# Attention scores of two experts as 64-row float32 products, with mask, scale and row minimum in one VectorE instruction

## The chip, the cores and the metric

The kernel runs on one core of a Trainium2 chip. The metric is the device time of one execution in microseconds (us).

## The reference, cut to what matters

Three layers follow one another: retention over 768 tokens (2 batches, 8 heads of 64), a feed-forward layer with 512 model columns and 2,048 hidden ones, and causal attention by four experts of head size 64, whose outputs are weighted by a gate that keeps the best two experts of each token. The change touches the attention alone:

```
scale = 1.0 / np.sqrt(Hd)
for e in range(E):
    q = x @ wq[e]
    k = x @ wk[e]
    v = x @ wv[e]
    scores = scale * (q @ k.transpose(0, 2, 1))
    causal = np.triu(np.ones((S, S), dtype=bool), 1)
    scores = np.where(causal, -1000000000.0, scores)
    scores = scores - scores.max(-1, keepdims=True)
    a = np.exp(scores)
    a /= a.sum(-1, keepdims=True) + 1e-09
    ye = a @ v @ wo[e]
```

## The kernel before, in words

The program is a list of steps (matmul groups, copies, transfers), each with an estimated cost, the buffers it reads and writes, and a priority. `Plan.issue` places them by a list schedule over estimated times when the program is built: a step is taken when its inputs are ready, its engine is free by the estimate and its new buffers have a place. The order found there is fixed for each engine; on the chip an engine runs its list in that order and waits where an input is late. Names in `QUEUES` share one order of allocation, so that all score, probability and transposed tiles are handed out in program order.

The attention has these steps, all in the last quarter of the execution.

- `q_proj` (line 747) makes queries and keys of one block of 384 tokens (TB) for two experts at once: 12 matmuls of 128x384 into one PSUM bank, expert 2p on partitions 0 to 63, expert 2p+1 on 64 to 127. Each expert's half then goes to tiles of its own. A query tile `QS` holds in one half the query rounded to float32r (ScalarE, L766, times 0.125), in the other half the remainder (VectorE, L768). A key is kept as the rounded `KH` (ScalarE, L773) and the remainder `KL` (VectorE, L775), and a transfer within SBUF (L779) copies each to the other 64 partitions. So a product with 128 rows against `KH` and another against `KL` give the float32 product of 64 rows.
- `q_val` (L793) makes the values and gate logits of 128 tokens, `gates` the gates.
- `a_scores` (line 841) takes one tile `qt` of 128 queries and two experts (`z` = 0, 1): nk = 128(qt+1) keys, so 128 to 768 columns; above 512 columns in two halves in two banks (`ways` = 2). Per expert: matmuls L863 and L864 (against `KH` and `KL`), then on VectorE a `copy_predicated` L870 that writes -1e9 over the future part of the last 128 columns in PSUM, a `tensor_reduce` L871 for the negated row maximum, on ScalarE the exponential L873 from PSUM to the SBUF tile `pr`, with the row sum as accumulator (a second small instruction reads it out). After both experts, VectorE inverts the sums (L879, L880) and GpSimd multiplies `pr` by inverse and gate (L885).
- `a_turn` transposes `pr` in 128x128 pieces on TensorE (L905); `COPY` (L335, on whichever of ScalarE and VectorE is free by the plan) takes four pieces at a time from PSUM to `pt` or `ptn`.
- `a_value` multiplies by the values (L924; 64 output columns, two experts side by side), `a_out` by `wo` (L948), and the result goes out.

Batch 0's attention is interleaved with batch 1's projections (L756, L793). In the profile a matmul's form is written rows*columns of the stationary operand: 128*128 is the whole array, 128*64 (L924) uses half of its columns, 64*128 half of its rows. The retention scores at the start (L435) are plain float32 products with 64 rows, for two heads in alternation; each float32 product stands as two records.

Of the kernel before, what the change touches and what calls it, by code (L numbers as in the profile page):

```python
# [26 lines left out]
U32 = mybir.dt.uint32  # L27
AF = mybir.ActivationFunctionType
OP = mybir.AluOpType
# [28 lines left out]
ROUNDED = {"x", "w", "w1", "S", "t", "h", "wq", "wk", "wv", "wo", "qk0", "qk1", "at"}  # L58
# [149 lines left out]
def region(base, size, n, space="S"):  # L208
    return [(space, base + i * size, size) for i in range(n)]
# [3 lines left out]
def retention_channel_mlp_mixture_attention(ctx: ExitStack, tc: tile.TileContext, a):  # L213
# [13 lines left out]
    future = cst.tile([128, C], U32, name="future")  # L227
# [66 lines left out]
    PL["qk0"] = region(o_r, 3 * KB, 12)  # L294
    PL["vv0"] = region(o_r + 36 * KB, KB, 6)
    PL["ob"] = region(o_r + 42 * KB, 2 * KB, 2)
    PL["qk1"] = region(o_h, 3 * KB, 12)
    PL["vv1"] = region(o_h + 36 * KB, KB, 6)
    PL["pr"] = region(o_xt, 3 * KB, 8)
    PL["pt"] = region(o_x, 6 * KB, 3)  # L300
    PL["ptn"] = region(o_x, 7 * KB // 2, 5)
# [13 lines left out]
    def new(n):  # L315
        return Buf(PL[n], n)
# [4 lines left out]
    def ACT(c, fn, r=(), w=()):  # L321
        P.add({"A": c}, lambda e: fn(), r, w)

    def DVE(c, fn, r=(), w=()):
        P.add({"V": c}, lambda e: fn(), r, w)
# [412 lines left out]
    QS, KH, KL, VV, LG, GT = {}, {}, {}, {}, {}, {}  # L738
    xkeys = lambda t: [(t, "k", k) for k in range(NK)]

    def q_alloc(b):
        for e in range(E):
            QS[b, e], KH[b, e], KL[b, e] = (new(f"qk{b}") for _ in range(3))
        for t in range(NC):
            VV[b, t] = new(f"vv{b}")

    def q_proj(b, j, n, p):
# [12 lines left out]
        for z in range(2):  # L760
            e = 2 * p + z
            own = slice(64 * z, 64 * z + 64)
            oth = slice(64 - 64 * z, 128 - 64 * z)
            if n == "wq":
                q = QS[b, e]
                ACT(0.39, lambda q=q, own=own: act.activation(f32r(q)[own, cs], f32(pa, TB)[own], AF.Copy, scale=0.125),  # L766
                    r=[pa], w=[(q, j, 0)])
                DVE(0.47, lambda q=q, own=own, oth=oth: dve.scalar_tensor_tensor(  # L768
                    f32r(q)[oth, cs], f32(pa, TB)[own], 0.125, f32(q)[own, cs], op0=OP.mult, op1=OP.subtract),
                    r=[pa, (q, j, 0)], w=[(q, j, 1)])  # L770
            else:
                kh, kl = KH[b, e], KL[b, e]
                ACT(0.39, lambda t=kh, own=own: act.activation(f32r(t)[own, cs], f32(pa, TB)[own], AF.Copy),  # L773
                    r=[pa], w=[(kh, j, 0)])
                DVE(0.47, lambda t=kl, h=kh, own=own: dve.tensor_tensor(f32r(t)[own, cs], f32(pa, TB)[own],  # L775
                                                                        f32(h)[own, cs], OP.subtract),
                    r=[pa, (kh, j, 0)], w=[(kl, j, 0)])
                for t in (kh, kl):
                    DMA(96e3, lambda t=t, own=own, oth=oth: sp.dma_start(f32(t)[oth, cs], f32(t)[own, cs]),  # L779
                        r=[(t, j, 0)], w=[(t, j, 1)])  # L780
# [60 lines left out]
    def a_scores(b, qt, p):  # L841
# [3 lines left out]
        PR = []  # L845
        P.bias -= (20, 40)[b]
        for z in range(2):
            e = 2 * p + z
            s, pr = new("ps2" if nk > 512 else "ps1"), new("pr")
            PR.append(pr)  # L850

            ways = 1 if nk <= 512 else 2
            wide = nk // ways

            def halves(ap, step):
                return ap[:, :ways * step].rearrange("p (a x) -> p a x", a=ways)[:, :, :wide]

            def mm(e=e, s=s):
                q = f32r(QS[b, e])[:, qt * C:(qt + 1) * C]
                for n in range(ways):  # L860
                    ks = slice(n * wide, (n + 1) * wide)
                    out = f32(s)[:, 512 * n:512 * n + wide]
                    pe.matmul(out, lhsT=q, rhs=f32r(KH[b, e])[:, ks], start=True, stop=False)  # L863
                    pe.matmul(out, lhsT=q, rhs=f32r(KL[b, e])[:, ks], start=False, stop=True)  # L864
            PE(2 * ways * max(0.107, wide * .4513e-3 + .015), mm, r=[(QS[b, e], j, 0), (QS[b, e], j, 1)] +
               [(t, jj, y) for t in (KH[b, e], KL[b, e]) for jj in range(j + 1) for y in range(2)], w=[s])

            def mx(s=s, z=z):
                end = 512 * (ways - 1) + wide
                dve.copy_predicated(f32(s)[:, end - C:end], future, negs)  # L870
                dve.tensor_reduce(f32(sm)[:, z:z + 1], halves(f32(s), 512), axis=mybir.AxisListType.XY, op=OP.max, negate=True)  # L871
            DVE(0.43 + nk * 1.05e-3, mx, r=[s, "future", "negs"], w=[s, (sm, z)])
            ACT(act_c(nk) + .18, lambda s=s, pr=pr, z=z: act.activation(  # L873
                halves(f32(pr), wide), halves(f32(s), 512), AF.Exp, bias=f32(sm)[:, z:z + 1], scale=1.0,
                accum_out=f32(sm)[:, 2 + z:3 + z]), r=[s, (sm, z)], w=[pr, (sm, 2 + z)])
# [104 lines left out]
    DMA(64e3, lambda: sp.dma_start(future, a["future"]), w=["future"])  # L980
# [32 lines left out]

    load_mw("wv")
# [37 lines left out]
def _layouts(q, k, v, moe_g_ln, moe_w_ch1, moe_w_ch2, moe2_w_gate, moe2_wq, moe2_wk, moe2_wv, moe2_wo):  # L1052
# [12 lines left out]
    def f64_bits(w):  # L1065
# [16 lines left out]
        "future": (r[:, None] < r[None, :]).astype(np.uint32),  # L1082
# [26 lines left out]
```

## Time and profile before

| | |
|---|---|
| timed runs | 452.49 us median of 3 (452.15 to 453.15) |
| span of the profiled execution | 450.3 us (the page gives it no time of its own; the timed runs lie 1.8 to 2.8 us above that span) |
| PE (matmul) busy | 439.8 us, 98% of the span |
| DVE, ACT, POOL busy | 328.0, 223.4, 209.4 us |
| granted TensorE clock | 1.000 of full speed |
| chain that ended last | PE 86%, DVE 5%, DMA 3%, issue 2% |

The chain is the work followed back from the last instruction, at each step to what released it. Retention fills the first 75 us, the feed-forward layer lasts until about 317 us, the projections and the attention take the rest. Within the attention PE is busy nearly all the time, and short idle times before L905, L863 and L756 are put down to ScalarE and VectorE.

### The profile page before, as it was taken

To read this page: it belongs to the slowest core of one execution; us is meant where nothing else is said; L and a number is where in the kernel's file an instruction comes from. 1 tells how busy PE (TensorE), PEld (TensorE's weight loads), DVE (VectorE), ACT (ScalarE), POOL (GpSimd) and SP (SyncE) were. 2 spreads that over 40 slices of the span, in tenths; PEclk is the share of its full clock that TensorE was granted. 3 is DMA by queue.
4 is the path that set the end of the run, shared out by engine and by line. 5 is a ranking of instruction groups with operands and counts; after the bars stand their busy time and mean duration, and the time that the engine had idled before them with its cause. 6 is when DMAs were issued, how large, how long until landed. Compare 5 with 4: busy or idle time off the path is not lost.

```text
span 450.3 us, 8468 instructions
## 1 busy us (share of the span) xinstructions
PE 439.8 (98%) x3198; PEld 415.5 (92%) x3198; DVE 328.0 (73%) x709; ACT 223.4 (50%) x467; POOL 209.4 (47%) x216
## 2 busy tenths in 40 slices
PE   8999999999999999999999999999999999998996
PEld 7778889999999999999999999999999987897875
DVE  2798786868659767877868565569657988878962
ACT  1476566263256335344354164245534756645852
POOL 1688768978989325226155064100401333224440
PEclk9999999999999999999999999999999999999999
DMA  7998923203103104114021002003230220101111
GB/s 263 366 347 325 314 81 108 95 24 118 47 1 140 48 1 134 55 48 140 1 89 53 1 1 93 2 0 95 70 72 20 66 71 33 49 1 47 49 49 47
DMA packets 15129, 40.11 MB, mean 89 GB/s; under 512 B 2288, under 2 KB 4976, under 8 KB 15088
## 3 DMA queue, kind: packets, MB, share of 16 engines
q1 hardware_dynamic: 15088, 39.57, 26.0%
q8 instruction: 25, 0.41, 0.4%
q14 instruction: 16, 0.13, 0.1%
HBM read 33.27 MB, written 3.15 MB: 81 GB/s over the span
## 4 chain that ended last, share of the span: by engine, by line
PE 86%; DVE 5%; DMA 3%; issue 2%; ACT 1%; POOL 1%; SPq 1%; DVEq 0%; ACTq 0%; POOLq 0%
PE ps L611 29%; PE ps L672 19%; PE ps L592 8%; PE ps L756 6%; PE ps L924 4%; PE ps L793 4%; PE ps L905 4%; PE ps L948 3%; DMA vk<-in_vk_dram 3%; PE ps L486 2%; PE ps L863 2%; PE ps L864 2%; PE ps L463 2%; PE ps L435 1%; DVE sm L871 1%
## 5 line engine op out<-in xcount | busy, mean ns | idle before, releaser
L611 PE MATMUL ps<-h,w 128*128 128x384 f32 x768 | 145.6, 335 | 0.7 <-DVE xT L615 0.4
L611 PEld LDWEIGHTS ps<-h,w 128*128 128x128 f32 x768 | 134.0, 188 | 1.4 <-DVE xT L615 0.7
L615 DVE TENSOR_TENSOR xT<-xT,ps 128x384 f32<-128x384 f32 x112 | 60.1, 549 | 36.9 <-PE ps L611 36.6
L885 POOL TENSOR_SCALAR pr<-pr,sm,gate 128x384 f32<-128x384 f32 (+5 forms) x48 | 34.9, 738 | 80.4 <-DVE ps L870 32.8
L548 POOL TENSOR_TENSOR w<-wy,w 128x512 fp32r<-128x512 f32 x26 | 33.7, 1301 | 44.2 <-PE ps L611 39.7
L672 PE MATMUL ps<-t,S 128*128 128x384 f32 x216 | 43.1, 334 | 0.0
L873 ACT ACTIVATE pr<-ps,sm 128x384 f32<-128x384 f32 (+5 forms) x48 | 30.3, 636 | 20.8 <-DVE sm L871 15.5
L679 ACT ACTIVATE u<-ps 128x384 f32<-128x384 f32 x36 | 17.6, 490 | 41.4 <-PE ps L672 35.7
L672 PEld LDWEIGHTS ps<-t,S 128*128 128x128 f32 x216 | 37.9, 188 | 0.1
L592 PE MATMUL ps<-x,w 128*128 128x384 f32 x192 | 34.8, 336 | 0.4 <-ACT wx L523 0.4
L523 ACT ACTIVATE wx<-raw 128x512 f32<-128x512 f32 x32 | 21.5, 672 | 27.5 <-DVE ps L527 19.7
L592 PEld LDWEIGHTS ps<-x,w 128*128 128x128 f32 x192 | 33.2, 188 | 0.8 <-ACT wx L523 0.6
L871 DVE TENSOR_REDUCE sm<-ps 128x1 f32<-128x384 f32 (+5 forms) x48 | 30.0, 624 | 2.9
L524 POOL TENSOR_SCALAR wx<-wx 128x512 f32<-128x512 f32 x32 | 20.3, 633 | 18.5 <-ACT wx L523 17.7
L687 ACT ACTIVATE h<-ps 128x384 fp32r<-128x384 f32 x36 | 17.6, 490 | 22.6 <-PE ps L611 14.4
L672 PE MATMUL ps<-x,w 128*128 128x384 f32 x144 | 28.8, 334 | 0.0
L672 PEld LDWEIGHTS ps<-x,w 128*128 128x128 f32 x144 | 25.3, 188 | 0.0
L905 PE MATMUL ps<-ident,pr 128*128 128x128 f32 x168 | 22.5, 275 | 2.0 <-DVE at L935 1.2
L547 ACT ACTIVATE w<-wy 128x512 fp32r<-128x512 f32 x26 | 16.3, 627 | 16.4 <-PE ps L611 16.1
L525 DVE TENSOR_SCALAR ps<-wx 128x512 uint32<-128x512 uint32 x32 | 22.0, 686 | 2.2 <-POOL wx L524 1.8
L529 DVE SCALAR_TENSOR_TENSOR wy<-raw,ps 128x512 uint32<-128x512 uint32 x32 | 21.8, 682 | 1.9 <-POOL w L548 1.3
L527 DVE SCALAR_TENSOR_TENSOR ps<-wx,ps 128x512 uint32<-128x512 uint32 x32 | 22.3, 696 | 1.1
(123 smaller groups left out, 877.3 us busy)
## 6 DMA issues: line engine op xcount, KB each, us to landing
raw<-in_w_dram SPq DMA_DIRECT2D x32, 512.0 KB, 3.5
kq<-in_kq_dram SPq DMA_DIRECT2D x11, 512.0 KB, 5.5
vk<-in_vk_dram SPq DMA_DIRECT2D x11, 512.0 KB, 5.1
qk<-qk SPq DMA_DIRECT2D x32, 96.0 KB, 2.1
out_dram<-ob SPq DMA_DIRECT2D x11, 256.0 KB, 2.0
tabY<-in_tabY_dram SPq DMA_DIRECT2D x6, 256.0 KB, 5.2
vraw<-in_wv_dram SPq DMA_DIRECT2D x1, 520.0 KB, 3.6
kq<-in_kq_dram SPq DMA_DIRECT2D x2, 256.0 KB, 2.9
```

The lines of the kernel that those rows point to most:

```text
L525: DVE(0.62, lambda: dve.tensor_scalar(u32(z), u32(x), 4, 1, op0=OP.logical_shift_left, op1=OP.logical_shift_right), r=[x], w=[z])
L527: DVE(0.7, lambda: dve.scalar_tensor_tensor(u32(z), u32(x), 0x80000000, u32(z), op0=OP.bitwise_and, op1=OP.bitwise_or), r=[x, z], w=[z])
L548: POOL(1.34, lambda: pool.tensor_tensor(f32r(l), f32(y), f32(h), OP.subtract), r=[y, h], w=[l])
L592: pe.matmul(f32(pa, TB), lhsT=wt, rhs=blk(f32r(xt[b][j]))[:, k], start=(n == 0), stop=(n == 11))
L611: pe.matmul(f32(pa, TB), lhsT=wt, rhs=t, start=(n == 0), stop=(n == 5))
L615: DVE(0.55, lambda: dve.tensor_tensor(blk(f32(xt))[:, k], blk(f32(xt))[:, k], f32(pa, TB), OP.add), r=[pa] + [(xt, cc, w) for cc in range( ...
L672: pe.matmul(f32(pa, TB), lhsT=wt, rhs=t, start=(first and n == 0), stop=(n == 5), skip_group_check=True)
L756: pe.matmul(f32(pa, TB), lhsT=mw(n, lo, k, p * 128, (p + 1) * 128), rhs=blk(f32r(xt))[:, k], start=(i == 0), stop=(i == 11))
L871: dve.tensor_reduce(f32(sm)[:, z:z + 1], halves(f32(s), 512), axis=mybir.AxisListType.XY, op=OP.max, negate=True)
L873: ACT(act_c(nk) + .18, lambda s=s, pr=pr, z=z: act.activation(halves(f32(pr), wide), halves(f32(s), 512), AF.Exp, bias=f32(sm)[:, z:z + 1] ...
L885: POOL(0.28 + nk * 0.95e-3, lambda pr=pr, z=z, e=e: pool.tensor_scalar(f32(pr, nk), f32(pr, nk), f32(sm)[:, 6 + z:7 + z], GT[b, j][:, cc, ...
L905: pe.transpose(f32(pa)[:, i * C:(i + 1) * C], f32(PRS[z][x])[:, j * C:(j + 1) * C], ident)
```

## The change

The tiles `QS`, `KH`, `KL` go. `q_proj` copies its whole PSUM bank, both experts, in one `COPY` of 128x384 as plain float32 to `QT` or `KT`. There are no remainders, no scale and no transfers within SBUF.

`a_scores` multiplies the 64 partitions of one expert directly in float32 (line 838 of the changed kernel): for each half of the columns one product for z = 0 on rows 0 to 63 and one for z = 1 on rows 64 to 127, written to two different PSUM tiles. Both experts are one step that needs two score tiles and two `pr` tiles at once.

On VectorE a single `tensor_tensor_reduce` (L843) computes (score + mask) times -0.125 from PSUM and the SBUF tile `MASK`, writes it to `pr` in SBUF and gives the row minimum as accumulator, which a second small instruction reads out. The exponential (L846) then works in place on `pr` with scale -1. `MASK` holds zeros (a GpSimd memset of 128x640, new) and in its last 128 columns -8e9 for the future (the transfer of 64 KB, which was there before for `copy_predicated`, now queued before the load of `wv`). The room that the query and key tiles leave goes to four more `pr` and six more `ptn` places.

```
-ROUNDED = {"x", "w", "w1", "S", "t", "h", "wq", "wk", "wv", "wo", "qk0", "qk1", "at"}
+ROUNDED = {"x", "w", "w1", "S", "t", "h", "wq", "wk", "wv", "wo", "at"}
...
-    PL["qk0"] = region(o_r, 3 * KB, 12)
+    PL["qk0"] = region(o_r, 3 * KB, 4)
+    PL["mask"] = region(o_r + 12 * KB, 3 * KB, 1)
...
-    PL["qk1"] = region(o_h, 3 * KB, 12)
+    PL["qk1"] = region(o_h, 3 * KB, 4)
...
-    PL["pr"] = region(o_xt, 3 * KB, 8)
+    PL["pr"] = region(o_xt, 3 * KB, 8) + region(o_h + 12 * KB, 3 * KB, 4)
...
-    PL["ptn"] = region(o_x, 7 * KB // 2, 5)
+    PL["ptn"] = region(o_x, 7 * KB // 2, 5) + region(o_r + 15 * KB, 7 * KB // 2, 6)
...
-        for z in range(2):
-            e = 2 * p + z
...
-                for t in (kh, kl):
-                    DMA(96e3, lambda t=t, own=own, oth=oth: sp.dma_start(f32(t)[oth, cs], f32(t)[own, cs]),
-                        r=[(t, j, 0)], w=[(t, j, 1)])
+        dst = (QT if n == "wq" else KT)[b, p]
+        COPY(TB, lambda: f32(dst)[:, cs], lambda: f32(pa, TB), [pa], [(dst, j)])
...
+        SC, PR = ([new(kind) for _ in range(2)] for kind in ("ps2" if nk > 512 else "ps1", "pr"))
...
+        def mm():
+            for n in range(ways):
+                for z in range(2):
+                    own = slice(64 * z, 64 * z + 64)
+                    pe.matmul(f32(SC[z])[:, 512 * n:512 * n + wide], lhsT=f32(QT[b, p])[own, qt * C:(qt + 1) * C],
+                              rhs=f32(KT[b, p])[own, n * wide:(n + 1) * wide], start=True, stop=True)
+        PE(0.05 + nk * 1.667e-3, mm, r=[(QT[b, p], j)] + [(KT[b, p], jj) for jj in range(j + 1)], w=SC, hold=PR)
         for z in range(2):
...
+            s, pr = SC[z], PR[z]
+            DVE(0.2 + nk * 1.05e-3, lambda s=s, pr=pr, z=z: dve.tensor_tensor_reduce(
+                halves(f32(pr), wide), halves(f32(s), 512), halves(f32(MASK)[:, S - nk:], wide), -0.125, 3e38,
+                op0=OP.add, op1=OP.min, accum_out=f32(sm)[:, z:z + 1]), r=[s, (MASK, 0), (MASK, 1)], w=[pr, (sm, z)])
+            ACT(act_c(nk) + .18, lambda pr=pr, z=z: act.activation(
+                f32(pr, nk), f32(pr, nk), AF.Exp, bias=f32(sm)[:, z:z + 1], scale=-1.0,
+                accum_out=f32(sm)[:, 2 + z:3 + z]), r=[pr, (sm, z)], w=[pr, (sm, 2 + z)])
...
+    MASK = new("mask")
+    POOL(0.8, lambda: pool.memset(f32(MASK)[:, :S - C], 0.0), r=["seven"], w=[(MASK, 0)])
+    DMA(64e3, lambda: sp.dma_start(f32(MASK)[:, S - C:], a["future"]), r=["seven"], w=[(MASK, 1)])
...
+        "future": np.where(r[:, None] < r[None, :], 8 * NEG, 0).astype(np.float32),
```

The planner's new costs and buffers put the attention's steps in another order from there on; the first 1,594 rows of PE's list, up to the projections of batch 0, stay as they are. Two places show the kind of move. (In these rows the numbers behind a name tell buffers apart; x2 counts like instructions in a row.)

TensorE, batch 1, the scores of query tiles 2 and 3 (384 and 512 columns), before:

```order
L905 MATMUL ps<-ident,pr_4388 128x128
L905 MATMUL ps<-ident,pr_4410 128x128 x2
L863 MATMUL ps<-qk_530_3783,qk_543_3853 128x384
L864 MATMUL ps<-qk_546_3881,qk_543_3853 128x384
L905 MATMUL ps<-ident,pr_4402 128x128
L905 MATMUL ps<-ident,pr_4437 128x128 x2
L863 MATMUL ps<-qk_531_3786,qk_544_3864 128x384
L864 MATMUL ps<-qk_548_3885,qk_544_3864 128x384
L863 MATMUL ps<-qk_530_3783,qk_543_3853 128x512
L864 MATMUL ps<-qk_546_3881,qk_543_3853 128x512
L924 MATMUL ps<-ptn_4527,vv_596_4339 64x256
```

The scores of a single expert stand between groups of other matmuls, all of them of the form 128*128 apart from L924. The same place after the change:

```order
L838 MATMUL ps<-qk_519_3697,qk_534_3780 128x384 x2
L838 MATMUL ps<-qk_519_3697,qk_534_3780 128x512 x2
L878 MATMUL ps<-ident,pr_4027 128x128
L878 MATMUL ps<-ident,pr_4104 128x128 x2
L878 MATMUL ps<-ident,pr_4046 128x128
L878 MATMUL ps<-ident,pr_4112 128x128 x2
L878 MATMUL ps<-ident,pr_4223 128x128
L878 MATMUL ps<-ident,pr_4230 128x128 x2
L878 MATMUL ps<-ident,pr_4227 128x128
L878 MATMUL ps<-ident,pr_4246 128x128 x2
L838 MATMUL ps<-qk_525_3723,qk_557_3970 128x384 x2
L838 MATMUL ps<-qk_525_3723,qk_557_3970 128x512 x2
```

L838 are the score products (x2: both experts), L878 is the transpose that was L905. Both experts' scores now stand together, two query tiles in a row, and each such group is a stretch in the form 64*128 between stretches in 128*128.

VectorE, batch 0, the row maxima of the first score tiles, before (`sm` holds a tile's small columns):

```order
L870 COPY_PREDICATED ps<-future,negs 128x128
L871 TENSOR_REDUCE sm_3724<-ps 128x1
L870 COPY_PREDICATED ps<-future,negs 128x128
L871 TENSOR_REDUCE sm_3757<-ps 128x1
L879 TENSOR_SCALAR sm_3724<-sm_3724 128x2
L880 RECIPROCAL sm_3724<-sm_3724 128x2
L870 COPY_PREDICATED ps<-future,negs 128x128
L871 TENSOR_REDUCE sm_3757<-ps 128x1
```

and after the change:

```order
L843 ISA pr_3695,sm_3673<-ps,mask_3381 128x384
L843 ISA sm_3673 128x1
L843 ISA pr_3699,sm_3700<-ps,mask_3381 128x512
L843 ISA sm_3700 128x1
L843 ISA pr_3705,sm_3700<-ps,mask_3381 128x512
L843 ISA sm_3700 128x1
L852 TENSOR_SCALAR sm_3673<-sm_3673 128x2
L853 RECIPROCAL sm_3673<-sm_3673 128x2
```

Two instructions per expert stay two, but the second is a read-out of one column; the score tile in PSUM is done with after the first.

## Rows read from the trace of the kernel before

**Rows 1.** The page, busy time of each engine (us, share of the span, instructions).

```profile
PE 439.8 (98%) x3198; PEld 415.5 (92%) x3198; DVE 328.0 (73%) x709; ACT 223.4 (50%) x467; POOL 209.4 (47%) x216
```

**Rows 2.** Windows of the attention: start and end, length, engines' busy time, PE clock, DMA.

```profile
345.00:405.00 60.00, 59.11 (x423) 52.40 (x422) 50.75 (x143) 38.63 (x106) 19.52 (x29) 1.00 0.16 45
405.00:430.00 25.00, 23.61 (x168) 19.70 (x167) 22.26 (x66) 18.10 (x45) 12.06 (x17) 1.00 0.12 43
```

**Rows 3.** Groups of instructions, the page: busy us, mean ns, idle before them.

```profile
L871 DVE TENSOR_REDUCE sm<-ps 128x1 f32<-128x384 f32 (+5 forms) x48 | 30.0, 624 | 2.9
```

**Rows 4.** Groups of instructions by form, VectorE, 315 to 451 us.

```profile
L870 DVE COPY_PREDICATED ps<-future,negs 128x128 f32<-128x128 uint32 x48 | 17.4, 362 | 1.2 <-PE ps L864 0.5 <-PE ps L863 0.5
...
L775 DVE TENSOR_TENSOR qk<-ps,qk 64x384 fp32r<-64x384 f32 x16 | 8.9, 554 | 4.4 <-ACT qk L773 3.9
...
L935 DVE TENSOR_TENSOR at<-ps,at 128x256 fp32r<-128x256 f32 x11 | 4.5, 417 | 3.3 <-ACT at L933 3.3
...
L871 DVE TENSOR_REDUCE sm<-ps 128x1 f32<-128x256 f32 x8 | 3.4, 424 | 0.4
```

**Rows 5.** Groups of instructions by form, ScalarE, 315 to 451 us.

```profile
L873 ACT ACTIVATION_READ_ACCUMULATOR pr<-ps,sm 128x1 f32 x48 | 9.5, 198 | 0.0
L773 ACT ACTIVATE qk<-ps 64x384 fp32r<-64x384 f32 x16 | 7.8, 486 | 8.1 <-PE ps L756 7.1 <-DVE qk L775 0.8
```

**Rows 6.** Timeline, PE, a value stretch between scores (start us, us, line, form, count).

```profile
362.22 0.33 PE L863 MATMUL ps<-qk,qk 128*128 128x384 f32 x1
...
362.40 0.34 PE L864 MATMUL ps<-qk,qk 128*128 128x384 f32 x1
...
362.66 1.73 PE L924 MATMUL ps<-ptn,vv 128*64 128x256 f32 x16
...
364.33 0.44 PE L863 MATMUL ps<-qk,qk 128*128 128x384 f32 x1
...
364.61 0.33 PE L864 MATMUL ps<-qk,qk 128*128 128x384 f32 x1
```

**Rows 7.** Timeline, PE, a stretch of 64-row float32 products in the retention.

```profile
25.64 0.60 PE L486 MATMUL ps<-ident,xT 128*128 128x128 f32 x4
...
30.09 0.66 PE L486 MATMUL ps<-ident,xT 128*128 128x128 f32 x4
30.68 1.16 PE L435 MATMUL ps<-kq 64*128 64x128 f32 x16
31.77 0.66 PE L486 MATMUL ps<-ident,xn 128*128 128x128 f32 x4
```

**Rows 8.** Timeline, PE, scores of a tile with 128 columns.

```profile
378.71 0.27 PE L863 MATMUL ps<-qk,qk 128*128 128x128 f32 x1
378.82 0.27 PE L864 MATMUL ps<-qk,qk 128*128 128x128 f32 x1
```

**Rows 9.** Timeline, PE and its weight loads: idle time before it, in brackets.

```profile
323.71 2.04 PEld L756 LDWEIGHTS ps<-x,wk 128*128 128x128 f32 x12 [0.47 <-DVE qk L768]
...
373.52 1.42 PE L905 MATMUL ps<-ident,pr 128*128 128x128 f32 x11 [0.59 <-ACT pt L335]
...
382.32 0.66 PE L905 MATMUL ps<-ident,pr 128*128 128x128 f32 x4 [0.29 <-DVE pt L335]
...
416.23 0.63 PE L905 MATMUL ps<-ident,pr 128*128 128x128 f32 x4 [1.17 <-DVE at L935]
...
424.76 0.42 PE L863 MATMUL ps<-qk,qk 128*128 128x320 f32 x1 [0.22 <-ACT pr L873]
```

**Rows 10.** Timeline, SyncE, GpSimd and weight loads around the new mask.

```profile
309.40 0.33 SPq L729 DMA_DIRECT2D vraw<-in_wv_dram  x1
...
316.47 2.40 POOL L731 TENSOR_TENSOR wo<-mraw,wo 128x1024 fp32r<-128x1024 f32 x1 [33.48 <-ACT wo L730]
318.96 2.44 POOL L731 TENSOR_TENSOR wv<-vraw,wv 128x1040 fp32r<-128x1040 f32 x1
...
325.81 1.50 PEld L793 LDWEIGHTS ps<-wv,x 128*128 128x128 f32 x12
```

More of the change, by code (lines that the diff above doesn't have):

```diff
@@ L226, in retention_channel_mlp_mixture_attention @@
     before = cst.tile([128, E, E], F32, name="before")
-    future = cst.tile([128, C], U32, name="future")
     negs = cst.tile([128, C], F32, name="negs")
@@ L736, in mw @@
         return f32r(l if lo else h)[:, k * w + c0:k * w + c1]
-    QS, KH, KL, VV, LG, GT = {}, {}, {}, {}, {}, {}
+    QT, KT, VV, LG, GT = {}, {}, {}, {}, {}
     xkeys = lambda t: [(t, "k", k) for k in range(NK)]
     def q_alloc(b):
-        for e in range(E):
-            QS[b, e], KH[b, e], KL[b, e] = (new(f"qk{b}") for _ in range(3))
+        for p in range(2):
+            QT[b, p], KT[b, p] = (new(f"qk{b}") for _ in range(2))
         for t in range(NC):
@@ L759, in q_proj @@
             PE(0.98, mm, r=list(MW[n][:2]) + xkeys(xh) + xkeys(xl) + ["seven"], w=[pa])
-        for z in range(2):
-            e = 2 * p + z
[L762 to L777, printed above, removed]
-                for t in (kh, kl):
-                    DMA(96e3, lambda t=t, own=own, oth=oth: sp.dma_start(f32(t)[oth, cs], f32(t)[own, cs]),
-                        r=[(t, j, 0)], w=[(t, j, 1)])
+        dst = (QT if n == "wq" else KT)[b, p]
+        COPY(TB, lambda: f32(dst)[:, cs], lambda: f32(pa, TB), [pa], [(dst, j)])
     def q_val(b, t):
@@ L844, in a_scores @@
         sm = new("sm")
-        PR = []
         P.bias -= (20, 40)[b]
-        for z in range(2):
[L848 to L875, printed above, removed]
@@ new lines, in a_scores, with halves @@
+        ways = 1 if nk <= 512 else 2
+        wide = nk // ways
+        SC, PR = ([new(kind) for _ in range(2)] for kind in ("ps2" if nk > 512 else "ps1", "pr"))
+        def halves(ap, step):
+            return ap[:, :ways * step].rearrange("p (a x) -> p a x", a=ways)[:, :, :wide]
+        def mm():
[4 more added lines that the diff above has]
+                              rhs=f32(KT[b, p])[own, n * wide:(n + 1) * wide], start=True, stop=True)
@@ L979, in retention_channel_mlp_mixture_attention @@
             P.bias -= 40
-    DMA(64e3, lambda: sp.dma_start(future, a["future"]), w=["future"])
     DMA(8e3, lambda: sp.dma_start(before, a["before"]), w=["before"])
@@ L1081, in _layouts @@
         "caus": (r[:, None] <= r[None, :]).astype(np.float32),
-        "future": (r[:, None] < r[None, :]).astype(np.uint32),
+        "future": np.where(r[:, None] < r[None, :], 8 * NEG, 0).astype(np.float32),
         "ident": np.eye(C, dtype=np.float32),
```

## The prediction

> **What bounds the kernel now.** I read the page's busy times first: PE works 98% of the span [rows 1]. Then the windows of the attention, because the change begins only there: in 345 to 405 us PE is busy 59.1 of 60 us, in 405 to 430 us 23.6 of 25, always at a granted clock of 1.00, the 2.4 GHz level, while VectorE has 50.8 of 60 and 22.3 of 25 [rows 2]. So the attention is as long as PE's list of matmuls plus the times at which PE waits for VectorE and ScalarE. The timeline of PE shows five such waits in its brackets, 2.7 us together [rows 9]. A matmul's record is longer than the step to the next one (0.34 against 0.17 or 0.18 us, [rows 6]), so a bracket hides about 0.16 us of each wait; with five times that, the waits cost PE about 3.5 us. Hence two questions: does PE's own list become shorter or longer, and how much of the 3.5 us goes?
>
> **PE's columns.** Let nk be a tile's number of keys. Over 2 batches, 2 pairs of experts and 6 tiles, nk adds up to 4 x 128 x 21 = 10,752. Before, each pair takes four passes over nk columns (two experts, `KH` and `KL`). After, a 64-row float32 product is two records. In the retention 16 records, 8 products of 128 columns, are started within 1.16 - 0.27 = 0.89 us (0.27 is the record of one 128-column matmul) [rows 7, 8]. That is 0.11 us for each two records, one for either half of the rows: two passes of 128 columns at 2.4 GHz are 0.107 us. So the two heads do run side by side, and a pair of products costs four passes over nk, the same as before: 17.9 us both times.
>
> **PE's fixed cost per matmul.** Before there are 128 score matmuls. At 384 columns the step is 0.175 us [rows 6] where the columns take 0.160: 15 ns too much; at 128 columns it is 0.11 [rows 8] where they take 0.053: 57 ns. Sixteen of the matmuls have 128 columns, for the other 112 I take 15 ns: 0.9 + 1.7 = 2.6 us. After, 64 steps of two records cost some 6 ns over their columns [rows 7]: 0.4 us. This **saves 2.2 us**.
>
> **PE's changes of form.** This is the term that decides. When PE goes from 128*128 to 128*64 and back, the last step before the stretch is 0.26 instead of 0.175 us (+0.09), the stretch takes 1.67 us where its columns need 1.49 (twelve records of 256 columns and four of 128, two at a time: +0.18), and the first step after it is 0.28 instead of 0.175 (+0.11) [rows 6]. That is 0.38 us for two changes. For the form 64*128, which the change uses, the retention has the nearest rows: the stretch from 30.68 to 31.77 takes 1.09 us where its columns need 0.85 (+0.24), and the four transposes ahead of it, between two other stretches, 0.59 where four steps of (0.60 - 0.27)/3 = 0.11 make 0.44 (+0.15 for one entry and one exit) [rows 7]: 0.39 us for two changes. I take 0.19 us for each. In PE's order behind row 1,594 the form changes 18 times before (nine stretches of L924) and 44 times after: 18 stretches of L838, each of one or two tiles, come in, and seven of L897 are left. So 26 more changes **cost 4.9 us**. The bounds are 0.14 (entering L924 alone: 0.09, and 0.05 as its part of the 0.18) and 0.24, the whole surplus within the retention's stretch put down to one change: 3.6 to 6.2 us.
>
> [...]
>
> PE's list thus becomes 4.9 - 2.2 = 2.7 us longer.
>
> **VectorE and ScalarE.** Off go 48 `copy_predicated` (17.4 us) and 16 remainders of 0.55 us at L775 [rows 4], with 16 alike at L768: 35 us. The 48 reductions (30.0 us, [rows 3]) become 48 fused instructions. No row shows one. Nearest is L935, with one operand in PSUM, one in SBUF and the output in SBUF: 0.417 us at 256 columns, as the reduction's 0.424 [rows 4]; so 30 us again. Bounds: nothing cheaper than the reduction reads so many columns here; at the other end twice that, 60 us. The read-out costs at most what ScalarE's costs, 0.2 us [rows 5]: 48 x 0.2 = 9.6. Eleven of the 16 new bank copies stand on VectorE, at 0.55: 6 us. VectorE loses some 19 us of work. ScalarE loses 16 x 0.486 at L773 [rows 5] and 16 alike at L766, 15.6 us, and gains five copies. The exponential now reads SBUF, which I cost at nothing. None of this is on the path by itself: PE's list covers it, and it counts only through the waits.
>
> **Transfers, mask, GpSimd.** The 32 transfers within SBUF are off the path and stay worth nothing. The memset of 128x640 falls into the 33 us in which GpSimd is idle ahead of the split of `wo` [rows 10]. The mask's transfer stands on SyncE's queue ahead of `wv`, whose issue at 309.40 takes 0.33 us; a delay of that size is covered, since the split of `wv` ends at 321.4 and PE first uses it at 325.8. Were that cover of 4.4 us gone, PE would wait at L774, in nothing else's place.
>
> **The waits.** At 323.71 PE waits for the second of four small operations that free a projection's bank (0.47); one copy takes their place, so it goes. At 424.76 it waits for an exponential to free a score tile (0.22); that tile is now free after the fused instruction, so it goes. The other three, at transposes, wait for copies out of PSUM or for VectorE work queued ahead of them [rows 9], 2.05 us by the brackets and 2.5 in PE's steps. Less work on VectorE helps; but PE's new order has 24 transposes in one run in batch 0, whose seven copies compete with the maxima of the 768-column tiles. I let half of the 2.5 stay and add one new wait of the mean kind, 0.7: 2.0 us are left of 3.5. Bounds: none, and 5.
>
> **Sum**, against the profiled execution: +4.9 - 2.2 - 3.5 + 2.0 = **+1.2 us**, a span of 451.5. The median of the runs lies 2.2 us above the span, so 452.5 + 1.2 = **453.7 us**. A measurement of this kernel can tell about 0.2%, 0.9 us, from no change. The last 20 us, from the last scores on, keep their order and their length.
>
> **Rivals.**
> *PE runs dense, and the kernel gets faster.* All waits go, and a change of form costs 0.14 us: 3.6 - 2.2 - 3.5 = -2.1 us, 450.4. For it: the waits hang on VectorE, which is busy for 73 us in the two windows [rows 2] and loses 19 us over the attention. Against it: the retention's rows, where the form 64*128 itself costs 0.19. It decides as soon as changes and remaining waits together stay below 4.8 us. Chance 0.2.
> *The two cancel.* Changes at 0.19, but only about 0.8 us of waits left: 4.9 - 2.2 - 3.5 + 0.8 = 0, 452.5. Chance 0.3.
> *The fused instruction is slow.* At twice the reduction's time VectorE gets 30 us more and is as loaded as before or more; each pair's chain from scores to transposes grows by some 1.2 us. All waits stay, and two or three of the groups that wait now wait 1.2 us longer: 2.7 + 2.5 = +5.2, 457.7. Nothing in the trace speaks for or against a factor of two but L935. Chance 0.08. [...]
> *The change does not do what it says*: products of two experts do not run side by side at 320 to 512 columns. That adds 17.9 us: 471.6. The retention's rows speak against it. Chance 0.02.
>
> **How the numbers follow.** My own case (+1.2, between 453.4 and about 457) has 0.4, the rivals 0.2, 0.3, 0.08 and 0.02. Slower by over 0.2% is my case, the slow instruction and the serial products: 0.5. Same: 0.3. Faster: 0.2. The range leaves out the outer parts of both ends: from 450.8, most of the dense case, to 457.0, the sum with 5 us of waits (4.9 - 2.2 - 3.5 + 5 = +4.2) and a little above.
>
> **What would show it.** In the profile after: first steps into L838 of 0.2 us and 0.1 us lost on its second record, 18 such stretches; L838 in pairs of records a few ns apart; L843 of about 0.56 us at 384 columns; no L779; VectorE some 15 to 20 us less busy; remaining idle time of PE in front of L878. The prediction is wrong in its main term if a change costs under 0.15 us, in its second if PE's waits sum to under 1 or over 4 us.

## The result, and the profile after

The changed kernel takes 455.61 us (median of 6 runs, 454.75 to 456.21) where the kernel before took 453.21 in runs on the same chip (6 runs, 452.15 to 453.81). The ratio is 1.0053, 95% interval 1.0038 to 1.0069: slower by 0.5%, or 2.4 us. The profiled spans are 453.6 and 450.3 us. Of these 3.2 us, 0.65 stand ahead of the first projection matmul (L756 starts at 315.73 instead of 315.08), where the change does nothing; from there to PE's last start it is 133.64 us for 131.27, +2.4, as in the medians.

The busy times on the page of the changed kernel, to be read against [rows 1]:

```profile
PE 443.6 (98%) x3198; PEld 407.3 (90%) x3198; DVE 307.8 (68%) x698; ACT 206.2 (45%) x430; POOL 209.3 (46%) x217
```

VectorE lost 20 us and ScalarE 17, and the kernel became slower: PE, which has 98% of the span in both, is busy 3.8 us longer. The groups of the changed steps, on the page (busy us, mean ns, idle before them) and, for the last line, in the view of groups by form; to be read against [rows 3, 4]:

```profile
L846 ACT ACTIVATE pr<-pr,sm 128x384 f32<-128x384 f32 (+5 forms) x48 | 31.7, 663 | 14.4 <-DVE sm L843 14.3
...
L843 DVE CUSTOM_DVE_ANT_0 pr<-ps,mask 128x384 f32<-128x384 f32 (+5 forms) x48 | 28.2, 619 | 10.4 <-PE ps L838 8.1
...
L838 PE MATMUL ps<-qk,qk 64*128 64x384 f32 (+4 forms) x128 | 24.3, 474 | 0.5 <-DVE sm L843 0.5
```

```profile
L843 DVE DVE_READ_ACCUMULATOR2_ANT sm<- 128x1 f32 x48 | 4.0, 83 | 0.0
```

The fused instruction takes 619 ns on the mean, as the plain reduction did (624 in [rows 3]); mask and scale came free, at 83 ns for reading out the minimum. So the loss is not there. What PE does instead stands in its timeline (start us, us, line, form, count, idle time before it in brackets). First two undisturbed score stretches, then the part of the attention where it waits most:

```profile
353.49 1.56 PE L838 MATMUL ps<-qk,qk 64*128 64x384 f32 x8
354.98 0.33 PE L878 MATMUL ps<-ident,pr 128*128 128x128 f32 x1
...
357.85 1.35 PE L838 MATMUL ps<-qk,qk 64*128 64x320 f32 x8
359.12 3.25 PE L897 MATMUL ps<-ptn,vv 128*64 128x256 f32 x32
362.30 0.55 PE L878 MATMUL ps<-ident,pr 128*128 128x128 f32 x3
```

```profile
404.81 1.77 PE L838 MATMUL ps<-qk,qk 64*128 64x384 f32 x8
407.03 1.57 PE L878 MATMUL ps<-ident,pr 128*128 128x128 f32 x12 [0.44 <-POOL pr L858]
409.12 2.82 PE L838 MATMUL ps<-qk,qk 64*128 64x384 f32 x8 [0.52 <-DVE sm L843]
411.87 0.65 PE L897 MATMUL ps<-ptn,vv 128*64 128x256 f32 x4
```

Eight records of 384 columns, two at a time, need 1.28 us (within the stretch at 353.49 a pair takes 0.32 us from start to start); the stretch at 353.49 lasts 1.49 until the next start, 0.21 more. At 357.85 the stretch goes over into another form straight away and again has 0.20 on top of its columns (1.27 for 1.07, at 0.27 a pair). The 18 stretches are the predicted number, and 15 of them carry 0.21 us each. But the stretches at 404.81 and 409.12 hold the same work (384 and 512 columns), and the first is undisturbed inside (such a stretch takes 1.70 us to the next start, as at 341.08), while the second takes 2.75. Its bracket shows 0.52 us; another 1.05 us are lost inside it, where PE's own rows have no bracket. The rows of its weight loads have them, one for each of the four products:

```profile
409.12 0.29 PEld L838 LDWEIGHTS ps<-qk,qk 64*128 64x128 f32 x2 [0.75 <-DVE sm L843]
409.59 0.29 PEld L838 LDWEIGHTS ps<-qk,qk 64*128 64x128 f32 x2 [0.18 <-DVE sm L843]
410.21 0.29 PEld L838 LDWEIGHTS ps<-qk,qk 64*128 64x128 f32 x2 [0.32 <-DVE sm L843]
410.82 0.29 PEld L838 LDWEIGHTS ps<-qk,qk 64*128 64x128 f32 x2 [0.32 <-DVE sm L843]
```

To see where 2.4 us come from I added up PE's steps from one start to the next over single records, from the first L756 to the last start. Each record's own time is the step that undisturbed records of its kind show (0.174 us for 384 columns, 0.109 for a transpose, two passes for a pair in a narrow form), a change of form counts 0.2 us, and the rest is put down to waiting. Here for the kernels whose sums are used below:

| kernel | first to last start, us | own time | changes x 0.2 | rest |
|---|---|---|---|---|
| before | 131.27 | 123.97 | 18: 3.6 | 3.7 |
| after | 133.64 | 121.51 | 44: 8.8 | 3.3 |
| e1_fused_alone | 129.65 | 123.97 | 16: 3.2 | 2.5 |
| e2_products_alone | 138.24 | 121.51 | 45: 9.0 | 7.7 |
| e4_planner_told | 132.06 | 121.51 | 41: 8.2 | 2.4 |
| e6_gates_behind | 132.73 | 121.51 | 44: 8.8 | 2.4 |
| e8_fused_gates_behind | 130.99 | 123.97 | 16: 3.2 | 3.8 |
| e9_copies_on_ACT | 133.33 | 121.51 | 44: 8.8 | 3.0 |

The rest depends on the price put on a change: 0.01 us more takes 0.4 us off it in after and 0.2 in before. The single records bear it out: over the five waits of [rows 9] the steps of before are 3.3 us too long, and those of after are 3.1 us too long over five places between 406 and 428 us.

So after gains 2.5 us of own time, pays 5.2 us for 26 more changes, and gets only some 0.2 to 0.4 us of waiting back, although VectorE has 20 us less to do. The windows show where that work went. They compare equal times, at which the two kernels are at somewhat different steps: start and end, length, then busy us (x instructions) of PE, its weight loads, VectorE, ScalarE and GpSimd, clock, DMA. Before:

```profile
390.00:404.00 14.00, 14.00 (x107) 12.95 (x106) 10.76 (x45) 7.39 (x26) 2.17 (x5) 1.00 0.11 39
404.00:416.00 12.00, 11.06 (x78) 9.27 (x76) 10.70 (x38) 6.08 (x18) 5.31 (x10) 1.00 0.12 44
416.00:433.00 17.00, 16.55 (x111) 13.95 (x112) 15.21 (x36) 13.26 (x31) 9.11 (x11) 1.00 0.09 32
```

After:

```profile
390.00:404.00 14.00, 14.00 (x110) 12.64 (x107) 7.61 (x37) 4.14 (x15) 3.59 (x8) 1.00 0.10 39
404.00:416.00 12.00, 10.77 (x73) 6.23 (x72) 10.85 (x41) 7.73 (x24) 7.28 (x13) 1.00 0.01 1
416.00:433.00 17.00, 17.00 (x110) 11.99 (x110) 11.60 (x31) 9.39 (x22) 5.67 (x8) 1.00 0.17 63
```

Ahead of 404 us and behind 416 VectorE lost 3.2 and 3.6 us (10.76 to 7.61, 15.21 to 11.60), and behind 416 PE's rows now show it busy throughout. In between, where PE waits, VectorE is as busy as it was (10.70 and 10.85 of 12 us), and PE's busy time falls from 11.06 to 10.77. So VectorE's load fell where PE hardly waits now, and not where it waits; that this is the cause is tried below.

### The profile page after: what moved, and what is told of

Same layout as the page of the kernel before. It is cut to its first block, busy times and chain, and to the rows that moved or that the text cites. A ratio compares the mean times of both kernels' runs of the same rounds, so it can differ in the third digit from the quotient of the medians.

```text
span 453.6 us, 8298 instructions
## 1 busy us (share of the span) xinstructions
PE 443.6 (98%) x3198; PEld 407.3 (90%) x3198; DVE 307.8 (68%) x698; ACT 206.2 (45%) x430; POOL 209.3 (46%) x217
## 4 chain that ended last, share of the span: by engine, by line
PE 89%; DVE 4%; DMA 3%; issue 1%; ACT 1%; SPq 0%; POOL 0%; DVEq 0%; POOLq 0%
PE ps L611 28%; PE ps L672 19%; PE ps L756 8%; PE ps L592 7%; PE ps L897 4%; PE ps L838 4%; PE ps L774 4%; PE ps L878 4%; PE ps L921 4%; DMA kq<-in_kq_dram 2%; PE ps L435 2%; PE ps L486 2%; PE ps L463 1%; DMA gln<-in_gln_dram 1%; PE ps L454 1%
## 5 line engine op out<-in xcount | busy, mean ns | idle before, releaser
L846 ACT ACTIVATE pr<-pr,sm 128x384 f32<-128x384 f32 (+5 forms) x48 | 31.7, 663 | 14.4 <-DVE sm L843 14.3
L843 DVE CUSTOM_DVE_ANT_0 pr<-ps,mask 128x384 f32<-128x384 f32 (+5 forms) x48 | 28.2, 619 | 10.4 <-PE ps L838 8.1
L524 POOL TENSOR_SCALAR wx<-wx 128x512 f32<-128x512 f32 x32 | 20.2, 631 | 19.1 <-ACT wx L523 18.4
L838 PE MATMUL ps<-qk,qk 64*128 64x384 f32 (+4 forms) x128 | 24.3, 474 | 0.5 <-DVE sm L843 0.5
L878 PEld LDWEIGHTS ps<-ident,pr 128*128 128x128 f32 x168 | 18.6, 140 | 5.1 <-issue 2.4
```

The lines of the kernel that those rows point to most:

```text
L838: pe.matmul(f32(SC[z])[:, 512 * n:512 * n + wide], lhsT=f32(QT[b, p])[own, qt * C:(qt + 1) * C], rhs=f32(KT[b, p])[own, n * wide:(n + 1) * ...
L843: DVE(0.2 + nk * 1.05e-3, lambda s=s, pr=pr, z=z: dve.tensor_tensor_reduce(halves(f32(pr), wide), halves(f32(s), 512), halves(f32(MASK)[:, ...
L846: ACT(act_c(nk) + .18, lambda pr=pr, z=z: act.activation(f32(pr, nk), f32(pr, nk), AF.Exp, bias=f32(sm)[:, z:z + 1], scale=-1.0, accum_out ...
L878: pe.transpose(f32(pa)[:, i * C:(i + 1) * C], f32(PRS[z][x])[:, j * C:(j + 1) * C], ident)
```

## The experiments

The theory at the start: PE's own list sets the end, the changes of form cost what after loses, and the fused instruction helps. The rivals: the fused instruction or its read-out costs the time; or the changes are nearly free and something within the score stretches is slow. Ratios below are to the kernel before in the same runs.

### One half of the change at a time

The first kernel keeps the products of before and takes over the fused instruction with its mask and its exponential alone; the second is the changed kernel with the old steps behind its products (and the scale of 0.125 in the copy of the queries). The plan orders each of them anew, so a difference between two of these kernels holds the effect of another order too.

```diff
...
-                dve.copy_predicated(f32(s)[:, end - C:end], future, negs)
-                dve.tensor_reduce(f32(sm)[:, z:z + 1], halves(f32(s), 512), axis=mybir.AxisListType.XY, op=OP.max, negate=True)
...
+            DVE(0.2 + nk * 1.05e-3, lambda s=s, pr=pr, z=z: dve.tensor_tensor_reduce(
+                halves(f32(pr), wide), halves(f32(s), 512), halves(f32(MASK)[:, S - nk:], wide), -1.0, 3e38,
+                op0=OP.add, op1=OP.min, accum_out=f32(sm)[:, z:z + 1]), r=[s, (MASK, 0), (MASK, 1)], w=[pr, (sm, z)])
...
```

> The kernel before with the fused mask, scale and row minimum alone: the 128-row products of rounded queries and two-part keys stay, and only the VectorE and ScalarE instructions behind them change. Theory (PE's own list sets the end, and the changes of form of the 64-row products cost what after lost): PE's list keeps its products and makes 16 changes of form for 18 before, so 0.4 us come off, and the PE waits of 3.5 to 3.9 us shrink by 0 to 2 us because VectorE's work behind each score gets shorter: 450.5 to 453.0 us beside 453.2, ratio 0.994 to 1.000. Rival (the fused instruction or the read-out behind it is what made after slower): ratio 1.003 or more, 454.5 us and above.

Measured: 451.55 us, ratio 0.997 (0.9959 to 0.9982). It is faster than before and after, and stays so in a second set of runs:

> e1_fused_alone once more, unchanged, as the partner of e8: 451.0 to 452.0 us, ratio to before 0.996 to 0.998.

Measured: 451.63 us, ratio 0.9966 (0.9954 to 0.9978). The PE waits of e1 (line that waits, line waited for; total, times, longest):

```profile
PE ps L863 <- DVE sm L868: 0.4, 1, 0.4
PE ps L903 <- DVE qk L775: 0.2, 1, 0.2
```

Where the same view of before names four (1.2, 0.6, 0.3 and 0.2 us), it names two, and the long one on the `wo` remainder (1.17 us at 416.23) is gone. The fifth of [rows 9], on the weight load behind a projection, is in neither and stays 0.5 us in e1, which keeps the four small operations there. The rival that blames the fused instruction falls.

The other half:

```diff
...
-            DVE(0.2 + nk * 1.05e-3, lambda s=s, pr=pr, z=z: dve.tensor_tensor_reduce(
...
+                dve.copy_predicated(f32(s)[:, end - C:end], future, negs)
+                dve.tensor_reduce(f32(sm)[:, z:z + 1], halves(f32(s), 512), axis=mybir.AxisListType.XY, op=OP.max, negate=True)
...
```

> The changed kernel with its 64-row float32 products, but with the old steps behind them (predicated copy, row maximum, exponential from PSUM). Theory: the plain work falls by 2.4 us, 45 changes of form for 18 add 27 x 0.2 = 5.4 us, and the waits are those of after or longer, 3.4 to 5 us for 3.5 to 3.9: 455.5 to 458.2 us, ratio 1.005 to 1.011. Rival (the loss of after hangs on the fused instruction and its mask): at or under the kernel before, ratio up to 1.001.

Measured: 459.14 us, ratio 1.0134 (1.011 to 1.0158). Right in sign, but 1 us above the expected range: the waits were not 3.4 to 5 us but 7.7 (table). PE's waits of e2:

```profile
PE ps L844 <- ACT pr L854: 1.7, 2, 1.4
PE ps L886 <- POOL pr L866: 0.6, 1, 0.6
PE ps L886 <- ACT ptn L336: 0.4, 1, 0.4
```

A step here takes two score tiles at once and gets them only when ScalarE's exponential has read them out of PSUM. So the two halves together: with the products of before the fused steps save 0.3% (1.4 us); with the 64-row products they save 0.8% (1.0134 to 1.0053, about 3.6 us). The 64-row products cost 1.3% with the old steps and 0.8% with the fused ones (0.997 to 1.0053).

### More changes of form

```diff
             for n in range(ways):
+                if n:
+                    pe.matmul(f32(SC[0])[:, 512:544], lhsT=negs, rhs=negs[:, :32], start=True, stop=True)
                 for z in range(2):
```

> The changed kernel with one small 128-row product of 32 columns put between the two halves of each of the 8 two-half score tiles; its result is overwritten by a later product and used by nothing. It makes 16 more changes of form (60 for 44) and about 8 x 0.03 = 0.25 us of plain work. Theory (a change costs about 0.2 us): 16 x 0.2 + 0.25 = 3.4 us over after, bounds 2.2 to 4.8, that is 457.8 to 460.4 us, ratio to before 1.010 to 1.016. Rival (the changes are nearly free, and what the stretches lose lies in pairs that start apart or in waits): 0.3 to 0.8 us over after, ratio 1.006 to 1.007.

Measured: 459.70 us, ratio 1.0148 (1.0127 to 1.0168), 4.1 us over after by the medians and 4.3 by the ratios. The waits are the same as in after (0.5, 0.4 and 0.2 us by the view), so all of it is PE's list. Timeline of PE, a tile of 640 columns with the small product (L837) between its halves:

```profile
350.36 0.81 PE L840 MATMUL ps<-qk,qk 64*128 64x320 f32 x4
351.10 0.41 PE L837 MATMUL ps<-negs 128*128 128x32 f32 x2
351.44 0.81 PE L840 MATMUL ps<-qk,qk 64*128 64x320 f32 x4
352.18 0.33 PE L880 MATMUL ps<-ident,pr 128*128 128x128 f32 x1
```

The tile takes 1.82 us from first start to the transposes, where the one at 357.85 in after took 1.27: 0.55 us for two changes and the small product. Its two records would cost 0.22 at the least step that any row shows (0.11, [rows 8]) and 0.05 by their columns alone, which puts a change between 0.16 and 0.25 us. The theory holds, the rival is out.

### What keeps the waits

After's waits lie close together, from 404 to 416 us. Is it the plan? It counts 0.05 us beside a score step's columns, where two changes cost 0.4.

```diff
-        PE(0.05 + nk * 1.667e-3, mm, r=[(QT[b, p], j)] + [(KT[b, p], jj) for jj in range(j + 1)], w=SC, hold=PR)
+        PE(0.45 + nk * 1.667e-3, mm, r=[(QT[b, p], j)] + [(KT[b, p], jj) for jj in range(j + 1)], w=SC, hold=PR)
```

> The changed kernel with one number of the planner raised: a score step's PE cost from 0.05 to 0.45 us plus its columns, so that the plan counts the two changes of form that a step brings. The instructions are the same, their order differs from 315 us on, with 41 changes of form for 44. Theory (after's waits of 3.4 us are those of a plan that runs ahead of the engine): the waits fall by 1 to 2 us and three changes fewer save 0.6 us: 453.0 to 454.5 us, ratio to before 0.9995 to 1.003. Rival (the waits come from how batch 1 starts, whatever the plan's costs): within 0.6 us of after, ratio 1.004 to 1.007.

Measured: 453.39 us, ratio 1.0011 (0.9999 to 1.0024): 2.2 us below after by the medians, 1.9 by the ratios, and not to be told from before in these runs. Three changes fewer are 0.6 us, the rest of the waiting falls from 3.3 to 2.4 (table), and the first L756 starts 0.8 us earlier, which is no effect of the edit: in the two traces of e1, one and the same kernel, it starts at 314.8 and at 315.9 us. The one wait that its view keeps is the one on VectorE in front of the score step at 407.7 us, whose stretch again takes 2.75 us.

Why 2.75 and not 1.70? The single records show that the second expert's product starts 0.48 us behind the first. My theory then was that such a pair, once apart, pays twice. The edit lets both wait first:

```diff
+            if (b, qt, p) == (1, 2, 1):
+                for z in (1, 0):
+                    own = slice(64 * z, 64 * z + 64)
+                    pe.matmul(f32(SC[z])[:, :32], lhsT=f32(QT[b, p])[own, qt * C:(qt + 1) * C],
+                              rhs=f32(KT[b, p])[own, :32], start=True, stop=True)
```

> The kernel of e4_planner_told once more, unchanged, as the partner of e5_wait_together. Theory and rival alike: 453.0 to 454.0 us, within 0.3% of its first result, and in its trace the score stretch of 384 and 512 columns near 407.7 us again has its second expert's product 0.48 us behind the first and takes 2.75 us, where the same stretch without a lag takes 1.70.

Measured: 453.67 us, ratio 1.0012 (1.0002 to 1.0022), so e4 is some 0.1% slower than before. The 2.75 us stand there again.

> The kernel of e4_planner_told, and in the one score step near 407.7 us whose second product starts 0.48 us after the first, two small 64-row products of 32 columns go ahead, the second expert's first, into the first columns of the two PSUM tiles that the scores overwrite, so that both products of the pair begin only when both tiles are free. Theory (a pair that starts apart stays apart and pays the lag about twice): from the last transpose ahead of the step to the first product of probabilities and values behind it e4 takes 0.67 + 2.75 = 3.43 us; the step now starts 0.48 us later but runs in 1.70, with some 0.1 us for the small ones: 2.9 to 3.1 us, and the kernel's time is 0.3 to 0.5 us below e4's, ratio to it 0.999. Rival (the pair loses only the lag itself, so that starting both late wins nothing): 3.4 to 3.6 us there, and the time the same as e4's or up to 0.2 us above.

Measured: 453.76 us, ratio 1.0014 (1.0002 to 1.0025). The theory fell. PE's timeline, first of the partner, then of e5 (L838 there is the small pair, L843 the scores):

```profile
406.50 1.55 PE L878 MATMUL ps<-ident,pr 128*128 128x128 f32 x12
408.44 2.82 PE L838 MATMUL ps<-qk,qk 64*128 64x384 f32 x8 [0.39 <-DVE sm L843]
411.20 0.44 PE L897 MATMUL ps<-ptn,vv 128*64 128x256 f32 x2
```

```profile
406.00 1.55 PE L883 MATMUL ps<-ident,pr 128*128 128x128 f32 x12
408.43 0.41 PE L838 MATMUL ps<-qk,qk 64*128 64x32 f32 x4 [0.88 <-DVE sm L848]
408.67 2.10 PE L843 MATMUL ps<-qk,qk 64*128 64x384 f32 x8
410.70 0.65 PE L902 MATMUL ps<-ptn,vv 128*64 128x256 f32 x4
```

From the first transpose to the first product with the values it is 4.70 us in both. VectorE's timeline of e5 says what both wait for:

```profile
407.33 0.56 DVE L848 CUSTOM_DVE_ANT_0 pr<-ps,mask 128x384 f32<-128x384 f32 x1
...
407.81 0.55 DVE L848 CUSTOM_DVE_ANT_0 pr<-ps,mask 128x384 f32<-128x384 f32 x1
...
408.29 0.69 DVE L848 CUSTOM_DVE_ANT_0 pr<-ps,mask 128x512 f32<-128x512 f32 x1
...
408.90 0.69 DVE L848 CUSTOM_DVE_ANT_0 pr<-ps,mask 128x512 f32<-128x512 f32 x1
```

Four fused instructions of the step before run one behind the other and end at 407.9, 408.4, 409.0 and 409.6 us. Each frees one PSUM bank, and four products of the next step want these four banks: the small pair starts at 408.43, behind the second, and the last score product at 409.65, behind the fourth. So the pair does not pay for being apart. The stretch runs at VectorE's pace, bank by bank. In after, without the small pair, the same four stand behind the gates (L802 to L819):

```profile
404.63 0.24 DVE L802 TENSOR_TENSOR ga<-ga 128x48 f32<-128x48 f32 x1
...
408.38 0.17 DVE L819 TENSOR_TENSOR gate<-gate,ga 128x12 f32<-128x12 f32 x1
408.50 0.56 DVE L843 CUSTOM_DVE_ANT_0 pr<-ps,mask 128x384 f32<-128x384 f32 x1
...
408.98 0.55 DVE L843 CUSTOM_DVE_ANT_0 pr<-ps,mask 128x384 f32<-128x384 f32 x1
...
409.46 0.69 DVE L843 CUSTOM_DVE_ANT_0 pr<-ps,mask 128x512 f32<-128x512 f32 x1
...
410.07 0.69 DVE L843 CUSTOM_DVE_ANT_0 pr<-ps,mask 128x512 f32<-128x512 f32 x1
```

The four L843 end at 409.06, 409.53, 410.15 and 410.76 us, and the four weight loads shown above, each with its product, start some 0.06 us behind them.

What holds VectorE there are the gates of batch 1's second block (a dozen small instructions, in after from 404.6 to 408.5 us with two copies between them). Issued behind the four fused instructions, with PE's list of after:

```diff
...
+        late = [x for x in order if x[0].tag == ("gates", 1, 1)]
+        order = [x for x in order if x not in late]
+        at = next(i for i, x in enumerate(order) if x[0].tag == ("fused", 1, 3, 0, 1)) + 1
+        order[at:at] = late
         for n, e in order:
             n.fn(e)
...
```

> The changed kernel with PE's list unchanged; only the gate steps of batch 1's second block (13 small VectorE instructions and one ScalarE exponential) are issued behind the fourth fused mask and minimum of the score step near 404.8 us, where they stood ahead of the first. Theory (the waits that after keeps are VectorE's: the gates hold it until 408.5 us, and only then the four fused instructions free, one by one at 0.48, 0.48, 0.61 and 0.61 us, the PSUM banks that the next four products wait for): the 0.62 us ahead of the step near 409.1 us and the 1.05 us inside it go, perhaps also the 0.5 us at 407.0: 1.0 to 2.2 us below after, 453.4 to 454.6 us, ratio to before 1.001 to 1.003. Rival (the pair loses time by itself once it starts apart, or what is moved is late for POOL's scaling and the copies of transposed tiles instead): at most 0.4 us below after, 455.2 us and above, ratio 1.0045 or more.

Measured: 455.11 us, ratio 1.0045 (1.0033 to 1.0057): 0.4 us below after by the ratios, whose intervals overlap, and 0.9 us shorter in the trace (132.73 for 133.64). PE's timeline of e6 around the step (L846 scores, L888 transposes, L907 values), and the copy that it waits for in VectorE's timeline:

```profile
406.75 1.53 PE L888 MATMUL ps<-ident,pr 128*128 128x128 f32 x12
408.21 1.77 PE L846 MATMUL ps<-qk,qk 64*128 64x384 f32 x8
411.49 0.44 PE L907 MATMUL ps<-ptn,vv 128*64 128x256 f32 x2 [1.50 <-DVE ptn L341]
```

```profile
410.53 0.17 DVE L826 TENSOR_TENSOR gate<-gate,ga 128x12 f32<-128x12 f32 x1
...
410.89 0.54 DVE L341 COPY ptn<-ps 128x384 f32<-128x384 f32 x1
```

The mechanism is as the theory had it: both waits in front of the step and the 1.05 us inside it are gone, the stretch at 408.21 takes 1.7 us again. The size is the rival's: 1.5 us of a new wait stand behind it, for a copy that now queues behind the gates. The same on the plan of e4:

> e4_planner_told with the gates of batch 1's second block behind the same four fused instructions, PE's list that of e4. Theory: the 0.56 us ahead of the step near 407.7 us and the 1.05 us inside it go, 0.8 to 1.6 us below e4: 452.0 to 452.8 us, ratio to before 0.9965 to 1.000. Rival as for e6: within 0.3 us of e4, 453.2 to 453.9 us.

Measured: 453.15 us, ratio 1.0011 (1.0000 to 1.0021), the same as e4, with the same 1.5 us in front of the values. And on e1, whose longest wait (0.4 us in the view, 0.59 by the single records) hangs on the same gates:

> e1_fused_alone with the same gate steps behind the second fused instruction of the next step (the second one of 384 columns, which ran at 414.2 us, 1.2 us behind the first with the gates between them). PE's list is that of e1. Theory: the PE wait of 0.59 us at 414.8 us, whose bank that instruction frees, goes: 0.3 to 0.6 us below e1, 451.0 to 451.3 us, ratio to before 0.995 to 0.9965. Rival (the next wait, on the subtraction or on POOL's scaling, takes its place): within 0.2 us of e1.

Measured: 453.13 us, ratio 1.0013 (0.9999 to 1.0027), 1.5 us worse than e1 in the same runs, above the ranges of theory and rival. PE's waits of e8 (L913 transposes, L943 the subtraction for `wo`):

```profile
PE ps L913 <- DVE at L943: 1.5, 1, 1.5
PE ps L913 <- POOL pr L893: 0.2, 1, 0.2
```

0.6 us went, and 1.5 came at the subtraction behind the gates. Last, three copies off VectorE, first alone, then with the gates behind:

```diff
...
-            n.fn(e)
+            n.fn("A" if n.tag and n.tag[0] == "copy" and n.tag[1] == 1 and n.tag[2] == 0 else e)
...
```

> The changed kernel with PE's list and the order of all steps unchanged; the four copies of transposed probabilities of batch 1's first pair of tiles (384 columns each, near 406.3 to 411.6 us) run on ScalarE, where three of them ran on VectorE. Theory (between 404 and 412 us VectorE, busy 7.11 of 8 us, sets PE's pace, and ScalarE, busy 3.88, has room): two copies of 0.47 us no longer stand ahead of the four fused instructions and one no longer ahead of the product that waits for it: 0.6 to 1.3 us below after, 454.3 to 455.0 us, ratio to before 1.0025 to 1.004. Rival (the chain is one of dependences, and ScalarE's copies then stand ahead of its exponentials): within 0.3 us of after, ratio 1.0045 to 1.006.

Measured: 455.17 us, ratio 1.0055 (1.0041 to 1.0069): by the ratio no gain. PE's waits of e9 (L905 values):

```profile
PE ps L905 <- ACT ptn L337: 0.7, 1, 0.7
```

The copy that the values wait for now stands behind exponentials on ScalarE, as the rival had it, and the score step ahead of them (407.65 in e9) takes 2.82 us in PE's timeline as in after: the four banks still come free one by one.

> e6_gates_behind and the copies of e9 together, PE's list that of after. Theory: in e6 the two waits of 0.62 and 1.05 us were gone, and 1.5 us on a copy that stood behind the gates in VectorE's queue had come; with that copy on ScalarE, 0.2 to 0.6 us of it stay: 1.3 to 2.0 us below after, 453.6 to 454.3 us, ratio to before 1.0005 to 1.0025. Rival (the wait moves on once more): 454.8 us and above, 1.0035 or more.

Measured: 454.65 us, ratio 1.0037 (1.0022 to 1.0051), just above the theory's range and inside the rival's for the ratio: 0.7 us below after by the ratios, whose intervals overlap. What PE waits for in it stays open.

Taken together: what is moved in one queue removes the wait that it aims at (e6, e8), but another step then queues behind it, so that after gets back at most 0.7 us of its 3.3, which is not clear of the noise, and e1 loses 1.5. Only the whole plan anew (e4) gets about 2 us; one value of its cost was tried, so whether the truer price did it or merely another order is not shown. Which single chain would bring after's waits to nothing between 404 and 416 us is not settled. A plan in which score steps of one form follow each other was not tried. The best version is e1: the fused instruction with the products of before, 0.3% below the kernel before and 0.8% below the changed one.

## Why the prediction was right, and where a term was off

The forecast was slower, at +1.2 us; it is slower, at +2.4. Term by term:

- **PE's columns and fixed cost** (-2.2 us): -2.5 by the table (121.51 for 123.97). Right; the pairs run side by side at all widths (undisturbed, a pair of records takes 0.11 us from start to start at 128 columns, 0.22 at 256, 0.27 at 320, 0.32 at 384 and 0.43 at 512), so the rival of serial products is out. The forecast counts columns at 2.4 GHz. No page gives a frequency, only the granted clock as a share (1.000 before); the measured step of L924's pairs in the trace of before is 109 ns at 128 columns and 216 at 256. So two passes over 128 columns more take 107 ns, 2.4 columns a ns, which bears out the 0.107 us of the forecast.
- **Changes of form** (+4.9 us): 18 to 44 as counted, 0.2 us each in the 15 undisturbed stretches: +5.2. e3 bounds the price at 0.16 to 0.25 by itself. What PE does in that time no row shows.
- **The fused instruction** (the reduction's time, 30 us, and up to 0.2 us for the read-out): 28.2 us and 83 ns. Right, and the rival of twice the time is out. VectorE lost 20.2 us, predicted some 19. The exponential from SBUF, costed at nothing more, takes 31.7 us in all for 30.3 from PSUM, off the path.
- **The waits** (3.5 us, of which 2.0 left): this is the term that was mis-sized. The rest of PE's time is 3.3 us after, for 3.7 before (3.1 for 3.3 by the single records). The step that failed is the count of what stays: half of the 2.5 us at transposes, and one new wait of 0.7. All five waits of before went, more than was forecast, and five new ones of nearly the same sum came: 0.5 us at transposes behind GpSimd's scaling, 0.6 in front of and 1.05 inside one score step, which needs four banks that VectorE frees one by one, 0.7 at the values behind it, and 0.3 inside the score stretch at 427.27. "Less work on VectorE helps" held for the old waits; around the new ones the windows show its busy time as it was. The 1.2 us that separate +1.2 from +2.4 are this term, to the few tenths that the price of a change leaves open.
- **The dense rival** (-2.1 us) needed changes at 0.14 us and no waits; neither came. **The two cancel** needed 0.8 us of waits; there are 3.3. Its outcome is nearly reached by e4, whose plan counts 0.4 us for the changes of a score step: 3 changes and about a microsecond of waiting less, and 0.1% above before.

## What to carry to other kernels

Price a narrower matmul by how often it makes PE change its form, not by its columns alone: 26 changes took 5.2 us, where the narrower products saved 2.5. A plan that counts those changes did better here (e4). Work taken off an engine beside the path helped here only where the path waited for it: 20 us came off VectorE, but nothing between 404 and 416 us (10.85 us busy for 10.70), where PE waits, and PE got back only 0.2 to 0.4 us. Compare windows of its busy time around each wait before counting the saving. When a fused instruction and a new product come in one change, run them apart: here one is worth -0.3% and the other costs 0.8%.

## What was not expected

- A step that wants several PSUM banks can wait several times inside one stretch, and PE's matmul rows put a bracket only at the first: 0.52 us shown, 1.05 more hidden in a stretch of 2.75 us (after, 409.12). Comparing equal stretches finds it, and the rows of the weight loads name all four waits.
- VectorE starts the next fused instruction while the last is still ending: at 384 columns they take 0.55 us each and start 0.48 us apart (e5, 407.33 and 407.81), with the read-out of 83 ns hidden beside the next one. ScalarE's read-out took 198 ns [rows 5].
- Going from one narrow form straight to the other (L838 to L897 at 359.12 in after) cost here what the other changes did: the value stretch takes 3.18 us where its columns need 2.99 at 2.4 a ns, 0.19 too much, as the 0.18 of the stretch between whole-array products [rows 6].
